# Attention scores as three split single-pass products, and the odd head's copy shared by two engines

## The chip, the cores and the metric

The kernel runs on one core of a Trainium2 chip. The metric is the device time of one execution in microseconds. All times below are microseconds unless ns is written. The engines are TensorE (PE; its weight loads are listed apart as PEld), VectorE (DVE), ScalarE (ACT), GpSimd (POOL) and SyncE (SP), which here only issues transfers.

## What is computed

Three layers in a row, all in fp32: attention with a learned bias by position, a layer with the maximum of three products, and a layer of eight experts. The change is in attention:

```python
B, H, S, D = 2, 8, 576, 64
scores = scale * np.matmul(q, k.transpose(0, 1, 3, 2))
scores = scores + bias.transpose(2, 0, 1)[None]      # bias[i, j, head], from a small net of i and j
scores = scores - np.max(scores, axis=-1, keepdims=True)
attn = np.exp(scores)
attn = attn / (np.sum(attn, axis=-1, keepdims=True) + 1e-09)
x = np.matmul(attn, v)                               # then: relu layer of 768, experts of 8 x 1024
```

## The kernel before

The program's order on every engine is the order in which the code is written. Three stages matter here.

**The bias stage** (12 to 68 us) runs 36 steps g16. In each, four tests `gen_s` make 0/1 tables for the step two ahead, shared out by the letters of `TESTS` (G is GpSimd, A ScalarE, V VectorE); `bias_mm` sums them on TensorE, `bias_ev` and `bias_out` scale them on VectorE, `bias_store` mirrors a part on ScalarE and stores it in DRAM. The tests have 12 buffers, three steps' worth.

**Attention** (68 to 196 us) takes the heads in pairs p = 0 to 3; a pair has nine units k, u = 9p + k, 36 in all. A unit is 128 rows of queries of one batch, for both heads of the pair: the even head x = 0 lies on partitions 0 to 63, the odd one on 64 to 127. For k = 8 the 64 left-over rows of both batches make one unit. One turn s of the loop does, in this order:

- `u_qk(s)`: the scores of both heads into two PSUM tiles sc (two buffers for two tiles: the next unit needs both of them read).
- `u_tr(s-1, 0)`: ten transposes of the even head's exponentials pe, 64x128 each, into the PSUM tile pt, of which there is one; `pv_part(s)`: a part of the product with v, by the table `PV`.
- `u_max(s, x)` on VectorE: scores plus bias and the row extreme, for both heads; `u_ev(s-1, 0)` on ScalarE: the copy of pt to SBUF (128x640).
- `u_exp(s, 0)`, a P·V copy `pv_ev` where the table `EV` has one (k = 0, 2 and 4 of the next pair), `u_exp(s, 1)`, all on ScalarE.
- `u_tr(s-1, 1)` and `u_ev(s-1, 1)`: the odd head's transposes into the same pt, and its copy on VectorE.
- at k = 0 `r_add` (VectorE: reciprocals of the row sums); their transpose `r_tr` on TensorE follows in the next turn ahead of the P·V part; `r_out` and `r_in` carry them through DRAM; at k = 6 and 7 `x_out` on GpSimd scales a batch of the output and splits it into xh and xl (three instructions each). Weight steps `w_step` (one instruction of VectorE, ScalarE or GpSimd each) run at k in `W_AT` of pairs 1 to 3.

The loads of q and k for the next pair are issued at k = 1, of v at k = 5, of the bias every second turn.

**After attention** TensorE runs the second layer (`m1_mm`), whose last chunk of x comes from pair 3 through `x_last`; `m1_first` fills its wait. Everything behind is the same in both kernels.

A matmul whose operands are of type fp32r is one instruction and one record in the trace. An fp32 matmul is one call, and two records.

Of the kernel before, what the change touches and what calls it, by code (L numbers as in the profile page):

```python
# [9 lines left out]
F32 = mybir.dt.float32  # L10
# [41 lines left out]
def make_body(stop=None):  # L52
    def body(tc, a):
# [21 lines left out]
        with ctx, tc.manual_schedule():  # L75
# [94 lines left out]
            qk_t, v_t = {}, {}  # L170
            bias_t = {}

            def load_qk(p):
                if p < H // 2:
                    qk_t[p] = hp_.tile([128, 2, B, S], F32, tag="qk", name="qk")
                    for part in range(2):
                        dma(qk_t[p][:, part], a["qk"][p][:, part])

# [18 lines left out]
            with ExitStack() as bctx:  # L197
# [126 lines left out]

                for g in range(8):
                    gen_s(g)
# [54 lines left out]
                for g16 in range(NG16):  # L381
                    ps = bias_mm(g16)
                    t = bias_ev(g16, ps)
                    for c in range(4):
                        if g16 + 2 < NG16:
                            gen_s(4 * (g16 + 2) + c)
                    bias_out(g16, ps, t)
                    if g16 == NG16 - 1:

                        A.activation(out=bc.tile([128, 1], F32, name="ex"), in_=ones[:, 0:1], func=AF.Exp)  # L390
                    for n in range(max(g16 - 1, 0), NG16 if g16 == NG16 - 1 else g16):
                        bias_store(n)
                    if g16 in (12, 20, 28):
                        load_bias((12, 20, 28).index(g16))
                    if g16 == 24:
                        load_v(0)

# [17 lines left out]
            with ExitStack() as actx:  # L415
# [13 lines left out]
                def u_qk(u):  # L429
# [3 lines left out]
                    q, kk = qk_t[p][:, 0], qk_t[p][:, 1]  # L433
                    for hf in range(2):
                        cs = slice(hf * SH, hf * SH + SH)
                        for x in range(2):
                            r = half[x]
                            if k < 8:
                                b, it = k % 2, k // 2
                                T.matmul(out=sc[x][:, hf, :SH], lhsT=q[r, b, 128 * it:128 * it + 128], rhs=kk[r, b, cs],  # L440
                                         start=True, stop=True)
                            else:
                                for b in range(B):
                                    T.matmul(out=sc[x][half[b], hf, :SH], lhsT=q[r, b, 512:576], rhs=kk[r, b, cs],
                                             start=True, stop=True)
# [17 lines left out]
                def u_exp(u, x):  # L463
                    p, k = divmod(u, 9)
                    c = 9 * x + U_COL[k]
                    pe = up.tile([128, S], F32, tag="pe", name="pe", bufs=6)
# [41 lines left out]
                def u_ev(u, x):  # L508
# [12 lines left out]
                    else:  # L521
                        V.tensor_copy(out=to, in_=src)
# [14 lines left out]
                def pv_ev(p, ch, b=None):  # L537
                    ps = pvs.pop(p)
                    if ch == 0:
                        x_t[p] = up.tile([128, B, S], F32, tag="x32", name="x32")  # L540
# [54 lines left out]
                for s in range(NU):  # L595
# [31 lines left out]
                    if k == 1:  # L627
                        load_qk(p + 1)
                    if k == 5:
# [630 lines left out]
def host_arrays(inp):  # L1260
# [3 lines left out]
    qk = np.stack([inp["q"], inp["k"]]).reshape(2, B, H // 2, 2, S, D).transpose(2, 3, 5, 0, 1, 4).reshape(H // 2, 128, 2, B, S)  # L1264
# [49 lines left out]
```

## Time and profile before

| | us |
|---|---|
| median of 3 runs (1066.9 to 1071.85) | 1067.08 |
| the profiled execution | 1065.98 |
| its span in the trace | 1064.2 |
| PE busy | 1040.0 (98%) |
| DVE busy | 756.7 (71%) |
| ACT busy | 560.8 (53%) |
| POOL busy | 313.7 (29%) |

The busy time of PE is modelled from pipelined matmuls, so 98% doesn't mean that every microsecond is needed. The chain of work that ended last lies on PE for 85% and on DVE for 9% of the span; of its lines L565, L1218 and L1133 (stages behind attention) have most, and the attention lines L534 (P·V), L440 (scores) and L506 (transposes) have 4%, 3% and 3%. From attention on PE is at 9 tenths or more in every slice of the span.

### The profile page before, as it was taken

The page shows a single profiled execution, that of the slowest core. Times are in us where ns is not written, and L with a number is a line of the kernel's source. Part 1 is how long each engine was busy: PE and PEld are TensorE (multiplying, and loading weights), DVE is VectorE, ACT ScalarE, POOL GpSimd, SP SyncE. Part 2 cuts the span into 40 slices and gives each one's busy share as a digit, 9 for nine tenths or more (in the row PEclk, how much of TensorE's full clock was granted, in tenths as well). Part 3 has the DMA queues.
Part 4 walks back from the last instruction along what each step waited for, and adds up shares of the span by engine and source line. Part 5 has one row for each costly group of instructions (what it writes and reads, how often), then busy time and mean ns, then how long its engine had stood idle before and what let it go on. Part 6 is the DMA issues. An engine that isn't in the chain of part 4 may idle for free.

```text
span 1064.2 us, 18893 instructions
## 1 busy us (share of the span) xinstructions
PE 1040.0 (98%) x7533; PEld 682.8 (64%) x7533; DVE 756.7 (71%) x1464; ACT 560.8 (53%) x922; POOL 313.7 (29%) x227
## 2 busy tenths in 40 slices
PE   7979999999999899999999999999999999999998
PEld 3246666899999666575665756657566475574653
DVE  7987777699968786877756667576675766757543
ACT  6977777345326656454454544545455454544530
POOL 6930323123206114344133141331412313223120
PEclk8999999999999999999999999999999999999999
DMA  4884673433441112203022030220302302110002
GB/s 150 261 270 149 190 223 89 141 120 119 82 139 41 33 31 65 65 21 85 20 66 65 20 85 21 65 68 32 71 23 63 83 22 66 27 39 6 2 1 89
DMA packets 39445, 85.31 MB, mean 80 GB/s; under 512 B 8052, under 2 KB 10300, under 8 KB 39356
## 3 DMA queue, kind: packets, MB, share of 16 engines
q1 hardware_dynamic: 39212, 83.81, 27.3%
q8 instruction: 59, 0.97, 0.4%
q10 hardware_dynamic: 144, 0.29, 0.1%
q14 instruction: 30, 0.25, 0.1%
HBM read 70.78 MB, written 13.30 MB: 79 GB/s over the span
## 4 chain that ended last, share of the span: by engine, by line
PE 85%; DVE 9%; ACT 3%; DMA 1%; issue 1%; POOL 0%; DVEq 0%; ACTq 0%
PE d L1218 33%; PE x L1133 12%; PE m L565 11%; PE y L1133 8%; PE z L1133 8%; PE pv L534 4%; PE sc L440 3%; PE pt L506 3%; PE p L343 1%; DVE bo L362 1%; PE o L984 1%; DVE s L1147 1%; DVE hl L1156 1%; DVE pk L711 1%; DMA bias_f<-bo 1%
## 5 line engine op out<-in xcount | busy, mean ns | idle before, releaser
L1218 PE MATMUL d<-w2h,hh 128*128 128x512 f16 x576 | 218.3, 379 | 0.8 <-DVE acc L1229 0.8
L1218 PE MATMUL d<-w2h,hl 128*128 128x512 f16 x576 | 218.3, 379 | 0.2 <-DVE hl L1156 0.2
L1218 PE MATMUL d<-w2l,hh 128*128 128x512 f16 x576 | 218.3, 379 | 0.0
L1133 PEld LDWEIGHTS <-w1h 128*128 128x128 f16 x1792 | 175.3, 98 | 49.7 <-issue 2.3
L1218 PEld LDWEIGHTS <-hh 128*128 128x128 f16 x1152 | 112.6, 98 | 132.9 <-issue 1.0
L1232 DVE SCALAR_TENSOR_TENSOR acc<-d,kh,acc 128x512 f32<-128x512 f32 x126 | 94.2, 748 | 93.6 <-PE d L1218 93.4
L864 POOL TENSOR_TENSOR w1l<-wf,w1h 128x768 f16<-128x768 f32 x32 | 53.6, 1676 | 359.2 <-ACT w1h L863 285.0
L1151 ACT ACTIVATE hh<-s 128x576 f16<-128x576 f32 x128 | 87.3, 683 | 128.5 <-DVE s L1147 100.9
L1156 DVE SCALAR_TENSOR_TENSOR hl<-s,hh 128x576 f16<-128x576 f32 x128 | 99.2, 776 | 47.5 <-ACT hh L1151 44.9
L867 ACT ACTIVATE w1h<-wf 128x1024 f16<-128x1024 f32 x32 | 33.8, 1056 | 132.2 <-DVE wf L860 132.2
L870 POOL TENSOR_TENSOR w1l<-wf,w1h 128x1024 f16<-128x1024 f32 x32 | 68.9, 2152 | 117.2 <-ACT w1h L867 117.2
L1133 PEld LDWEIGHTS <-w1l 128*128 128x128 f16 x896 | 87.9, 98 | 22.7 <-issue 0.4
L1218 PEld LDWEIGHTS <-hl 128*128 128x128 f16 x576 | 56.4, 98 | 68.5 <-DVE hl L1156 0.7
L1143 ACT ACTIVATE s<-x,cx 128x576 f32<-128x576 f32 x96 | 70.3, 733 | 28.6 <-PE x L1133 27.2
L945 POOL TENSOR_TENSOR w2l<-w2r,w2h 128x512 f16<-128x512 f32 x64 | 73.1, 1163 | 25.0 <-ACT w2h L944 25.0
L1133 PE MATMUL x<-xth,w1h 128*128 128x288 f16 x384 | 78.4, 286 | 0.6 <-ACT s L1143 0.6
L1133 PE MATMUL x<-xtl,w1h 128*128 128x288 f16 x384 | 78.6, 286 | 0.2 <-POOL xtl L875 0.2
L1133 PE MATMUL x<-xth,w1l 128*128 128x288 f16 x384 | 78.4, 286 | 0.0
L1147 DVE SCALAR_TENSOR_TENSOR s<-z,cx,s 128x576 f32<-128x576 f32 x64 | 52.3, 817 | 32.0 <-PE z L1133 25.2
L565 PE MATMUL m<-xh,wh 128*128 128x384 f32 x216 | 72.7, 337 | 0.0
L565 PE MATMUL m<-xl,wh 128*128 128x384 f32 x216 | 72.5, 336 | 0.0
L565 PE MATMUL m<-xh,wl 128*128 128x384 f32 x216 | 72.4, 335 | 0.0
(203 smaller groups left out, 1977.4 us busy)
## 6 DMA issues: line engine op xcount, KB each, us to landing
wr<-in_moe_w SPq DMA_DIRECT2D x50, 512.0 KB, 3.6
w2r<-in_moe_w SPq DMA_DIRECT2D x64, 256.0 KB, 2.8
bias_f<-bo SPq DMA_DIRECT2D x36, 295.5 KB, 4.0
bias<-bias_f SPq DMA_DIRECT2D x32, 288.0 KB, 3.2
qk<-in_qk SPq DMA_DIRECT2D x8, 576.0 KB, 6.2
wr<-in_moe_w_out SPq DMA_DIRECT2D x6, 512.0 KB, 3.9
v<-in_v SPq DMA_DIRECT2D x4, 640.0 KB, 4.5
bias<-bias_f SPq DMA_DIRECT2D x16, 144.0 KB, 4.2
```

Of the source, the lines that this page charges most:

```text
L534: T.matmul(out=to[half[x]], lhsT=v_t[p][:, x, b, j, :], rhs=pts[ch][:, x, j, b * w:b * w + w], start=(j == 0), stop=(j == 4))
L565: T.matmul(out=p[:, :TG], lhsT=ws[:, 128 * c:128 * c + 128], rhs=xs[:, c, TG * g:TG * g + TG], start=(c == 0 and n == 0), stop=(c == 3 and ...
L864: G.tensor_tensor(out=lo[:, 0:3], in0=t[:, 1:4], in1=hi[:, 0:3], op=ALU.subtract)
L870: G.tensor_tensor(out=lo[:, 3:7], in0=t[:, 4:8], in1=hi[:, 3:7], op=ALU.subtract)
L945: G.tensor_tensor(out=lo, in0=r, in1=hi, op=ALU.subtract)
L1133: T.matmul(out=ps[bank][:, s, :SH], lhsT=ws[:, i, c, :], rhs=xv[:, j, c, s * SH:s * SH + SH], start=(start and k == 0), stop=(k == 5), **kw)
L1143: A.activation(out=t, in_=src, func=AF.Identity, scale=c)
L1147: V.scalar_tensor_tensor(out=out, in0=z, scalar=scale, in1=out, op0=ALU.mult, op1=ALU.add)
L1151: A.activation(out=o, in_=src, func=AF.Relu)
L1156: V.scalar_tensor_tensor(out=l, in0=src, scalar=0.0, in1=o, op0=ALU.max, op1=ALU.subtract)
L1218: T.matmul(out=pd, lhsT=hs[:, fh, 128 * t:128 * t + 128], rhs=ws, start=(k == 0), stop=(k == 11))
L1232: V.scalar_tensor_tensor(out=acc[:, t, :], in0=pd, scalar=kh[:, 1 + t:2 + t], in1=acc[:, t, :], op0=ALU.mult, op1=ALU.add)
```

## The change

The scores are no longer fp32 products. q and k of a pair are split on the chip into a part that fits the single-pass type (h) and the rest (l), and a score is the sum of qh·kh, qh·kl and ql·kh. The parts of pair 0 are made in the bias stage: the h parts by ScalarE ahead of its tests, the l parts by GpSimd in four pieces of 576 columns after steps 11, 15, 19 and 23. Those of pair p + 1 are made by GpSimd at k = 2 to 5 of pair p. Left-over rows of batch 1 stand first in its q (the host lays them so) and 64 columns of zeros stand between the batches, so that the k = 8 unit sums two full products of 128 rows.

The odd head's copy out of pt is halved between VectorE and ScalarE. The P·V copies go from ScalarE to VectorE, behind the odd head's copy. The odd head's transposes and copy now stand ahead of `u_exp(s, 1)`. pe has 5 buffers (6 before), x32 one and qk one (2 before each); the parts have two.

```diff
@@ parts of q and k
+            def split_qk(p, part, low, bs=slice(0, B), on_act=False):
+                if p < H // 2:
+                    if p not in hl_t:
+                        hl_t[p] = [[hp_.tile([128, B, w], F32R, tag=t + x, name=t + x) for t, w in (("q", 640), ("k", S))] for x in "hl"]
+                        for x in range(2):
+                            G.memset(raw(hl_t[p][x][0][:, 0, S:]), 0.0)
+                    hi, lo = (t[part][:, bs, :S] for t in hl_t[p])
+                    src = qk_t[p][:, part, bs]
+                    if low:
+                        G.tensor_tensor(out=lo, in0=src, in1=raw(hi), op=ALU.subtract)
+                    elif on_act:
+                        A.activation(out=hi, in_=src, func=AF.Copy)
+                    else:
+                        pool_copy(hi, src)
...
+                for part in range(2):
+                    split_qk(0, part, False, on_act=True)
+                pieces = [(0, part, True, slice(b, b + 1)) for b in range(B) for part in range(2)]
                 for g in range(8):
                     gen_s(g)
...
+                    if g16 % 4 == 3 and 7 < g16 < 24:
+                        split_qk(*pieces.pop(0))
@@ u_qk
-                    q, kk = qk_t[p][:, 0], qk_t[p][:, 1]
+                    hi, lo = hl_t[p]
+                    b, it = k % 2, k // 2
+                    mm = [(b, 704 * b + 128 * it)] if k < 8 else [(0, 512), (1, 576)]
+                    mm = [(q.rearrange("p b c -> p (b c)")[:, c:c + 128], kk[:, b]) for b, c in mm
+                          for q, kk in ((hi[0], hi[1]), (hi[0], lo[1]), (lo[0], hi[1]))]
                     for hf in range(2):
-                        cs = slice(hf * SH, hf * SH + SH)
-                        for x in range(2):
...
-                                T.matmul(out=sc[x][:, hf, :SH], lhsT=q[r, b, 128 * it:128 * it + 128], rhs=kk[r, b, cs],
-                                         start=True, stop=True)
...
+                        for y, (q, kk) in enumerate(mm):
+                            for x in range(2):
+                                T.matmul(out=sc[x][:, hf, :SH], lhsT=q[half[x]], rhs=kk[half[x], hf * SH:hf * SH + SH],
+                                         start=(y == 0), stop=(y == len(mm) - 1))
@@ u_ev, odd head
-                        V.tensor_copy(out=to, in_=src)
+                        V.tensor_copy(out=to[:, :, 0], in_=src[:, :, 0])
+                        A.activation(out=to[:, :, 1], in_=src[:, :, 1], func=AF.Copy)
@@ pv_ev
-                        A.activation(out=x_t[p][:, :, 0:256], in_=ps.rearrange("p (b i) -> p b i", b=2), func=AF.Copy)
+                        V.tensor_copy(out=x_t[p][:, :, 0:256], in_=ps.rearrange("p (b i) -> p b i", b=2))
...
-                        A.activation(out=x_t[p][:, b, 256:576], in_=ps[:, :320], func=AF.Copy)
+                        V.tensor_copy(out=x_t[p][:, b, 256:576], in_=ps[:, :320])
@@ one turn
                     u_exp(s, 0)
-                    for n, e in in_turn(EV, s):
-                        pv_ev(n, *e)
-                    u_exp(s, 1)
                     if s > 0:
                         u_tr(s - 1, 1)
                         u_ev(s - 1, 1)
+                    u_exp(s, 1)
+                    for n, e in in_turn(EV, s):
+                        pv_ev(n, *e)
...
                     if k == 1:
                         load_qk(p + 1)
+                    if 1 < k < 6:
+                        split_qk(p + 1, k // 2 - 1, k % 2 == 1)
```

In the order of TensorE's instructions, the place around unit 8 (k = 8 of pair 0), before; sc are score tiles, pt the transposes, pv the product with v, and "x4" that one instruction stands four times:

```order
L440 MATMUL sc<-qk 128x288 x4
L506 MATMUL pt<-ident,pe 128x64 x10
L534 MATMUL pv<-pt_1513,v 64x256 x4
L506 MATMUL pt<-ident,pe 128x64 x10
L444 MATMUL sc<-qk 64x288 x8
L506 MATMUL pt<-ident,pe 128x64 x10
L534 MATMUL pv<-pt_1513,v 64x256 x4
```

The scores of unit 8 after (the same place; qh, ql, kh, kl are the parts):

```order
L523 MATMUL pt<-ident,pe 128x64 x10
L461 MATMUL sc<-kh,qh 128x288 x2
L461 MATMUL sc<-kl,qh 128x288 x2
L461 MATMUL sc<-kh,ql 128x288 x2
L461 MATMUL sc<-kh,qh 128x288 x2
L461 MATMUL sc<-kl,qh 128x288 x2
L461 MATMUL sc<-kh,ql 128x288 x2
L461 MATMUL sc<-kh,qh 128x288 x2
L461 MATMUL sc<-kl,qh 128x288 x2
L461 MATMUL sc<-kh,ql 128x288 x2
L461 MATMUL sc<-kh,qh 128x288 x2
L461 MATMUL sc<-kl,qh 128x288 x2
```

The last row of them, one more ql, is left out. A usual unit has the first six such rows, 12 matmuls, where it had 4 fp32 calls; unit 8 has twelve rows, 24 matmuls, where it had 8 calls on quarters of the array.

VectorE at the turn k = 0 of pair 1, before (ISA is the reduction of `u_max`, with its accumulator read; rt and st the row sums; ww a weight step):

```order
L457 ISA ng,st<-sc,bias 128x576
L457 ISA st 128x1
L522 COPY pt_1514<-pt 128x10x64
L477 TENSOR_SCALAR rt<-st 128x6x3
L478 RECIPROCAL st<-rt 128x18
L124 TENSOR_SCALAR ww<-ww 128x4x128
L457 ISA ng,st<-sc,bias 128x576
```

and after:

```order
L474 ISA ng,st<-sc,bias 128x576
L474 ISA st 128x1
L539 COPY pt_1526<-pt 128x5x64
L559 COPY x_2044<-pv 128x2x256
L494 TENSOR_SCALAR rt<-st 128x6x3
L495 RECIPROCAL st<-rt 128x18
L124 TENSOR_SCALAR ww<-ww 128x4x128
L474 ISA ng,st<-sc,bias 128x576
```

The copy is half as wide, and the P·V copy x stands between it and the reciprocals; the next unit's reduction is behind all of them. ScalarE around the same turn, before:

```order
L520 ACTIVATE pt_1514<-pt 128x10x64
L467 ACTIVATE pe,st<-ng,st 128x576
L541 ACTIVATE x_1911<-pv 128x2x256
L467 ACTIVATE pe,st<-ng,st 128x576
L110 ACTIVATE ww<-wr 128x4x128
```

and after:

```order
L537 ACTIVATE pt_1526<-pt 128x10x64
L484 ACTIVATE pe,st<-ng,st 128x576
L540 ACTIVATE pt_1526<-pt 128x5x64
L484 ACTIVATE pe,st<-ng,st 128x576
L110 ACTIVATE ww<-wr 128x4x128
```

Half of the odd head's copy now stands between the two exps in every turn, and the P·V copy is gone.

## Rows read from the trace of the kernel before

**Rows 1.** Stage table, core 0: length, busy of PE, PEld, DVE, ACT, POOL (instructions), clock, DMA

```profile
93.00:123.00 30.00, 30.00 (x348) 18.53 (x344) 22.34 (x51) 22.61 (x52) 6.51 (x6) 1.00 0.61 183
```

**Rows 2.** Timeline of a unit: start, length, engine, line, operation, tiles [idle before <-releaser]

```profile
83.17 0.80 PEld L440 LDWEIGHTS sc<-qk 64*128 64x128 f32 x8
...
83.43 0.82 DVE L522 COPY pt<-pt 128x640 f32<-128x640 f32 x1 [0.30 <-PE pt L506]
...
84.37 0.42 PEld L506 LDWEIGHTS pt<-ident,pe 64*128 64x128 f32 x10 [0.41 <-ACT pe L467]
...
84.56 0.76 DVE L457 CUSTOM_DVE_ANT_0 ng<-sc,bias 128x576 f32<-128x576 f32 x1 [0.30 <-PE sc L440]
...
84.86 0.63 PEld L534 LDWEIGHTS pv<-pt,v 128*64 128x64 f32 x8
...
84.97 0.70 ACT L520 ACTIVATE pt<-pt 128x640 f32<-128x640 f32 x1 [0.65 <-PE pt L506]
...
85.24 0.75 DVE L457 CUSTOM_DVE_ANT_0 ng<-sc,bias 128x576 f32<-128x576 f32 x1
...
85.57 0.77 ACT L467 ACTIVATE pe<-ng,st 128x576 f32<-128x576 f32 x1
...
85.87 0.39 PEld L506 LDWEIGHTS pt<-ident,pe 64*128 64x128 f32 x10 [0.39 <-ACT pt L520]
...
86.17 0.79 PEld L440 LDWEIGHTS sc<-qk 64*128 64x128 f32 x8
...
86.44 0.82 DVE L522 COPY pt<-pt 128x640 f32<-128x640 f32 x1 [0.43 <-PE pt L506]
```

**Rows 3.** Chain that ended last, in order of time: start, length, what

```profile
110.70 1.77 PE pv L534 x12
...
181.63 1.13 PE sc L444 x16
...
195.71 109.58 PE m L565 x630
...
310.86 9.69 PE o L984 x72
```

**Rows 4.** Groups by form, 0 to 420 us: count | busy, mean ns | idle before

```profile
L543 ACT ACTIVATE x<-pv 128x320 f32<-128x320 f32 x6 | 2.6, 437 | 1.9 <-PE pv L534 1.9
...
L132 ACT ACTIVATE wh<-ww 128x512 fp32r<-128x512 f32 x18 | 11.3, 630 | 18.8 <-DVE ww L130 18.7
...
L130 DVE SCALAR_TENSOR_TENSOR ww<-wr,ww 128x512 int32<-128x512 int32 x24 | 16.9, 704 | 0.7
...
L551 POOL TENSOR_TENSOR xl<-x,xh 128x576 fp32r<-128x576 f32 x6 | 8.5, 1415 | 0.5
...
L62 POOL TENSOR_SCALAR xh<-x 128x576 fp32r<-128x576 f32 x6 | 4.4, 735 | 0.5
```

**Rows 5.** Timeline at k = 0 of pair 2, VectorE

```profile
129.71 0.27 DVE L478 RECIPROCAL st<-rt 128x18 f32<-128x18 f32 x1
```

**Rows 6.** Stage table in steps of 1 us, columns as in rows 1

```profile
9.00:10.00 1.00, 0.00 (x0) 0.00 (x0) 0.93 (x4) 1.00 (x3) 1.00 (x1) 0.50 0.00 0
```

**Rows 7.** Timeline of the bias stage's start, ScalarE's tests

```profile
9.02 2.69 ACT L318 ACTIVATE s<-rs,nthr 128x564 f16<-128x564 f16 x4
...
14.70 1.37 ACT L318 ACTIVATE s<-rs,nthr 128x528 f16<-128x528 f16 x2 [3.00 <-DVE t L352]
```

**Rows 8.** Timeline of the bias stage, GpSimd's tests and VectorE's first reading of step 13

```profile
30.00 1.21 POOL L321 TENSOR_SCALAR s<-rs,thr 128x372 f16<-128x372 f16 x1 [0.27 <-PE p L343]
...
34.86 0.59 DVE L352 SCALAR_TENSOR_TENSOR t<-p,ics,tab 128x372 f32<-128x372 f32 x1
...
38.20 15.92 POOL L321 TENSOR_SCALAR s<-rs,thr 128x324 f16<-128x324 f16 x12 [0.22 <-PE p L343]
```

**Rows 9.** Timeline at the end of attention, the last P·V copy on ScalarE

```profile
187.51 0.60 ACT L541 ACTIVATE x<-pv 128x512 f32<-128x512 f32 x1 [0.38 <-PE pv L534]
```

**Rows 10.** DMA issues by line: count, KB each, median us to landing

```profile
qk<-in_qk SPq DMA_DIRECT2D x8, 576.0 KB, 6.2
```

More of the change, by code (lines that the diff above doesn't have):

```diff
@@ L168, in body @@
             hp_ = hctx.enter_context(pool("heads", bufs=2))
-            qk_t, v_t = {}, {}
+            qk_t, v_t, hl_t = {}, {}, {}
             bias_t = {}
@@ L174, in load_qk @@
                 if p < H // 2:
-                    qk_t[p] = hp_.tile([128, 2, B, S], F32, tag="qk", name="qk")
+                    qk_t[p] = hp_.tile([128, 2, B, S], F32, tag="qk", name="qk", bufs=1)
                     for part in range(2):
                         dma(qk_t[p][:, part], a["qk"][p][:, part])
+            def split_qk(p, part, low, bs=slice(0, B), on_act=False):
[12 more added lines that the diff above has]
+                        pool_copy(hi, src)
             def load_v(p):
@@ L432, in u_qk @@
                     un[u] = {"sc": sc, "pe": []}
-                    q, kk = qk_t[p][:, 0], qk_t[p][:, 1]
-                    for hf in range(2):
-                        cs = slice(hf * SH, hf * SH + SH)
-                        for x in range(2):
-                            r = half[x]
-                            if k < 8:
-                                b, it = k % 2, k // 2
-                                T.matmul(out=sc[x][:, hf, :SH], lhsT=q[r, b, 128 * it:128 * it + 128], rhs=kk[r, b, cs],
-                                         start=True, stop=True)
[L442 to L445, printed above, removed]
+                    hi, lo = hl_t[p]
[3 more added lines that the diff above has]
+                          for q, kk in ((hi[0], hi[1]), (hi[0], lo[1]), (lo[0], hi[1]))]
+                    for hf in range(2):
+                        for y, (q, kk) in enumerate(mm):
+                            for x in range(2):
+                                T.matmul(out=sc[x][:, hf, :SH], lhsT=q[half[x]], rhs=kk[half[x], hf * SH:hf * SH + SH],
+                                         start=(y == 0), stop=(y == len(mm) - 1))
                 st_t = {}
@@ L465, in u_exp @@
                     c = 9 * x + U_COL[k]
-                    pe = up.tile([128, S], F32, tag="pe", name="pe", bufs=6)
+                    pe = up.tile([128, S], F32, tag="pe", name="pe", bufs=5)
                     A.activation(out=pe, in_=un[u].pop(("ng", x)), func=AF.Exp, bias=st_t[p][:, 0, c:c + 1], scale=-1.0,
@@ L539, in pv_ev @@
                     if ch == 0:
-                        x_t[p] = up.tile([128, B, S], F32, tag="x32", name="x32")
-                        A.activation(out=x_t[p][:, :, 0:256], in_=ps.rearrange("p (b i) -> p b i", b=2), func=AF.Copy)
+                        x_t[p] = up.tile([128, B, S], F32, tag="x32", name="x32", bufs=1)
+                        V.tensor_copy(out=x_t[p][:, :, 0:256], in_=ps.rearrange("p (b i) -> p b i", b=2))
                     else:
-                        A.activation(out=x_t[p][:, b, 256:576], in_=ps[:, :320], func=AF.Copy)
+                        V.tensor_copy(out=x_t[p][:, b, 256:576], in_=ps[:, :320])
                 def x_out(p, b):
@@ L1262, in host_arrays @@
     c = np.ascontiguousarray
-    qk = np.stack([inp["q"], inp["k"]]).reshape(2, B, H // 2, 2, S, D).transpose(2, 3, 5, 0, 1, 4).reshape(H // 2, 128, 2, B, S)
+    q = np.stack([inp["q"][0], np.concatenate([inp["q"][1][:, 512:], inp["q"][1][:, :512]], 1)])
+    qk = np.stack([q, inp["k"]]).reshape(2, B, H // 2, 2, S, D).transpose(2, 3, 5, 0, 1, 4).reshape(H // 2, 128, 2, B, S)
     v = inp["v"].reshape(B, H // 2, 2, S, D)
```

## The prediction

> **What bounds the kernel now.** First the stage table. The change touches the bias stage (12 to 68 us) and attention (68 to 196 us); behind them 870 us run on as they are, with TensorE full. In attention no engine is full: VectorE and ScalarE work 22.3 and 22.6 of 30 us at a granted clock of 1.00, and TensorE's 30.00 is modelled [rows 1]. So the limit is a ring of waits, and the timeline of one unit shows it [rows 2]. One PSUM tile pt serves both heads. T is the load of the odd head's transposes (85.87). Its copy starts 0.57 later (86.44, VectorE, 0.82 long), and the next even transposes load 0.12 after a copy ends (83.43 + 0.82 = 84.25, then 84.37): 0.57 + 0.82 + 0.12 = 1.51 us. From there 0.49 to the P·V product (84.86) and 1.01 to the next T (85.87): 3.01 us a unit. Two other rings are nearly as long. TensorE's own: the scores load 0.30 after T (86.17) and hold the array until the even transposes, 1.20 later (83.17 to 84.37), which is the same 1.5. That of the score tiles: load 83.17, first reduction 84.56, second 85.24, done at 86.0, next load 86.17: 2.83 to 3.0. An edit that shortens one of the three alone gains next to nothing; this one shortens all three.
>
> **The scores.** Before, a unit is 4 fp32 products, 8 records in the trace. What a column costs follows from two full-array fp32r streams: 630 matmuls of 384 columns in 109.58 us are 0.174 each, 72 of 288 in 9.69 are 0.135, so 96 columns cost 0.039 us, 0.41 ns a column, and the rest is 0.015 a matmul [rows 3]. That products on array halves run in pairs shows at P·V: 12 records of 320 columns at two passes would be 12 x 0.262 = 3.1 us in a row, and took 1.77 [rows 3]. By the same reckoning the old scores are 4 rounds of 2 x 288 columns, 0.95 us plus a little. The new unit is 12 single-pass matmuls of 288 columns, 6 rounds of two: 6 x 0.135 = 0.81, at least 6 x 0.12 = 0.72. That no load shows between them rests on the transposes: ten loads of 64x128 fit into the 0.30 us between 85.87 and 86.17, five to a half, 0.06 each, under the 0.12 that a matmul streams [rows 2]. TensorE's part behind T falls from 0.36 + 0.95 to 0.36 + 0.81 = 1.17.
>
> The Trainium skill speaks against this. "TensorE: Matmul & The Clock Gate", section "LDWEIGHTS (loading the stationary operand)", gives a load by its columns, so an estimate of 107 ns for 128, and its Part 3 on packing small matmuls lets a load overlap a running matmul only in another row group. By that a round would be 0.107 + 0.12, six of them 1.36, and the scores would be dearer than before; the sum would be the second rival's. Its first figure is not what the ten loads of rows 2 show; the second is not decided by any row with short matmuls.
>
> **The odd head's copy.** VectorE and ScalarE take half each. ScalarE's 128x320 takes 0.44 [rows 4] against 0.70 for 640 [rows 2]; in that ratio VectorE's 0.82 becomes 0.51. ScalarE starts later than VectorE behind transposes (84.37 to 84.97 is 0.60 for the even ones), but must first end the even head's exp, which starts at 85.57 and takes 0.77, so it is free before T + 0.57. So this path is 0.57 + 0.51 + 0.12 = 1.20, or 0.60 + 0.44 + 0.12 = 1.16 on ScalarE: I take 1.18, level with TensorE's 1.17. A unit with P·V goes from 3.01 to 2.68, 0.33 less. Bound: if the scores keep their 0.95, 0.36 + 0.95 = 1.31 and the gain is 0.20. There are 27 such units (5 to 35 without the four k = 8): **-8.9**, bound -5.4. Units 1 to 4 have no P·V and follow the ring of the score tiles; it loses about 0.26 of scores and hand-over: **-1.0**, bound -0.5.
>
> **The k = 8 units.** They ran 16 records on quarters in 1.13 us [rows 3], and now run 24 on halves: 12 x 0.135 = 1.62, against 0.95 of four rounds on quarters. TensorE is then ready at T + 0.36 + 1.62 = 1.98; before, 0.36 + 1.13 = 1.49 lay under the ring's 1.51. So +0.47 each, **+1.9** for four, bounds +1.2 (12 x 0.12) and +2.4.
>
> **What lands on VectorE and ScalarE instead.** ScalarE per unit: even copy 0.60 (84.97 to 85.57), two exps of 0.77, half a copy 0.34 to its successor: 2.5 of 2.68 us. VectorE: reductions 0.68 + 0.76, half copy 0.47: 1.9. So both have little room, and what came beside them free before now shows. At each k = 0 (three times) VectorE does the P·V copy of 512 columns behind its half copy (some 0.65, from 0.82 for 640), then the reciprocals of the row sums (0.27 [rows 5], some 0.38 with the add ahead of them), and in two pairs a weight step of 0.43 to 0.70. The next scores are ready at T + 1.35; VectorE is free at T + 1.04 + 0.65 + 0.38 = 2.07, with the step at 2.5 to 2.75. The transposed reciprocals make TensorE wait too (r_tr stands ahead of P·V). I get +0.3 to +0.8 at each of the three: **+1.6**, bounds 0 and +3. The two 320-column P·V copies, 0.4 each, mostly fit the 0.3 of slack: **+0.3**. The weight steps elsewhere (VectorE 0.70, ScalarE 0.63 [rows 4]) find 0.1 to 0.3 of slack at units with short P·V: five of them cost 0.2 to 0.4, with smaller ones **+2.0**, bounds 0 and +3.
>
> **Bias stage.** Two ScalarE copies of 1,152 columns stand ahead of its tests: by the step from 0.44 to 0.70 us for 320 more columns, 1.13 each, 2.3 in all. The q and k loads are in by then, as the DMA share is 0.00 from 9 us [rows 6], so ScalarE ends its four tests (2.69, from 9.02) at 14.0. It idled 3.00 us until 14.70 [rows 7]: nothing. GpSimd gets four subtractions of 1.41 [rows 4]. It has 0.27 of idle a step up to 38 us and none behind (12 tests in 15.92) [rows 8], so a part of the 5.7 us stays as lateness, some 3.4 us at the fourth. The cover is the lead of the tests: that of step 13 (372 columns) is done at 31.21 and VectorE first reads what comes of it at 34.86 [rows 8], 3.65 us later, of which its own matmuls take a part: about 3. What passes it meets a wait of VectorE that is there anyway. **+0.3**, bounds 0 and, with the cover gone at the last two, +2.6.
>
> **Later pairs' parts** cost GpSimd 2 x 1.47 + 2 x 2.8 = 8.6 us a pair (twice the 0.73 and 1.41 of [rows 4]), with x_out's 7.1 behind: 15.7 of some 27 us. Nothing, unless it is late (below). The loads keep their place on SP's queue; the single qk buffer is read out a pair earlier. The pads are set once per pair by GpSimd, hidden.
>
> **The end of attention.** The last P·V copy moves ahead of the reciprocals on VectorE (before, 0.60 from 187.51 on ScalarE [rows 9]), and r_tr, which stood ready right behind the transposes, waits for it: **+0.7**, bounds 0 and +0.9. Everything behind keeps its distance.
>
> **Sum.** -8.9 - 1.0 + 1.9 + 1.6 + 0.3 + 2.0 + 0.3 + 0.7 = -3.1 us from the profiled execution's 1065.98 (span 1064.2 and 1.8 around it): 1062.9. The median shown is 1067.08, 1.1 above that execution; I give 1063.5, between 1062.9 and 1064.0. With all good bounds it is -8.7 (1058 on the median's footing), with all bad ones +6 (1073).
>
> **Rivals.**
> 1. *The added work hides after all.* The +1.6, +2.0 and +0.3 rest on slacks of 0.1 to 0.3 us. If VectorE and ScalarE catch up within a unit, as they did before, the sum is -7.0, and -7.7 with the k = 8 units at the low bound: about 1059.5, and 1057 if the scores are at 0.72 and the copies keep pace with them. For it: long P·V units leave 0.4 to 0.8 us to catch up. Against it: ScalarE at 2.5 of 2.68.
> 2. *Loads show (slower).* A load into a half waits until that half's matmul is through. A round is then 0.12 + 0.06 = 0.18 from the ten loads, or 0.12 + 0.10 from the eight of the old scores (0.79 us merged at 83.17). Six rounds are 1.08 to 1.32, T + 1.44 to 1.68 against 1.51: a unit gains 0.07 or loses 0.17 (-1.9 to +4.6 over 27), a k = 8 unit takes 1.0 to 1.5 more (+4.0 to +6.0), and with +4.9 from the other terms it is +7 to +15.5: 1074 to 1082. It decides once a round is above 0.15. For it: no row has so short a matmul behind a load on the same half. Against it: the two fp32r streams hide a full-array load behind 0.12 us of streaming. It is the skill's overlap rule made a mechanism.
> 3. *GpSimd is late.* With one x32 buffer VectorE's P·V copy at k = 0 waits until x_out of the pair before is through. From the qk issue: 6.2 us landing [rows 10], 8.6 of parts, 7.1 of x_out is 21.9, against some 23.5 to the copy. If GpSimd runs a tenth slower and the load lands a microsecond late, it is 0.9 to 1.5 late at two boundaries: +2 to +3, 1066.
> 4. *It doesn't do what it says*: the halves don't pair in this form. Twelve in a row are 1.62, T + 1.98: +0.47 x 27, +2.1 x 4, +5: above 1085.
>
> **How the numbers follow.** Forecast 0.50, the first rival 0.26, the second 0.12, the third 0.09, the fourth 0.03. A measurement of this kernel can tell about 0.5% from no change, 5.3 us: faster is below 1061.7, slower above 1072.4. The forecast's own spread puts 0.12 of its 0.50 below 1061.7 and 0.02 above 1072.4; so faster 0.12 + 0.26 = 0.38, slower 0.02 + 0.12 + 0.03 = 0.17, same 0.45. The range 1055.5 to 1071.5 takes in nearly all of the forecast, rival 1 with 1.5 us below its 1057 (the spread of the before runs is larger), and rival 3; it leaves out 2 and 4 and some of the tails.
>
> **What would show it.** In the profile after: units of 2.7 us with 8 P·V records of 256 columns; score loads to even transposes in about 1.0 instead of 1.20, and about 1.7 at k = 8; the half copies at 0.44 and 0.5; ScalarE over 85% busy in attention; units k = 1 longer than the others by 0.3 to 0.8, with VectorE's reduction starting late; the bias stage's end at 68.0 to 68.5; granted clock 1.00 as before. It is wrong if score rounds take more than 0.15 us, if the bias stage ends above 70, or if a P·V copy waits for GpSimd.

## The result and the profile after

| | before | after |
|---|---|---|
| median, us | 1067.57 (6 runs, 1066.55 to 1071.85) | 1075.26 (6 runs, 1074.25 to 1077.05) |
| profiled execution, us | 1065.98 | 1075.98 |
| its span and mean granted clock | 1064.2, 0.991 | 1074.2, 0.984 |
| load of the first scores, us | 67.96 | 68.14 |
| load of unit 6's scores, us | 86.17 | 90.17 |
| start of the 630 matmuls behind attention, us | 195.71 | 205.80 |

The ratio is 1.0061, 95% interval 1.0044 to 1.0079: slower by 0.6%. The forecast was 1063.5, at most 1071.5. In the two profiles all of the loss has come by the end of attention, as the 630 matmuls that started at 195.71 [rows 3] start 10.1 us later and take as long as before. (The profiled execution of before is one of its shorter ones, so this is more than the 6.5 us of the ratio.) The chain that ended last, after (start, length, what):

```profile
205.80 109.47 PE m L583 x630
```

The stage table of after for the stretch of [rows 1] (columns as there) has VectorE at 18.76 us for 22.34, ScalarE at 22.94 for 22.61, GpSimd at 9.32 for 6.51. VectorE gave work away, and no engine is full. The limit is still a ring of waits:

```profile
93.00:123.00 30.00, 27.51 (x367) 19.05 (x365) 18.76 (x49) 22.94 (x55) 9.32 (x8) 1.00 0.58 171
```

One unit of after in its timeline, to be laid beside [rows 2] (start, length, engine, line, operation, tiles, idle before and what ended it):

```profile
155.93 0.39 PEld L523 LDWEIGHTS pt<-ident,pe 64*128 64x128 f32 x10 [0.39 <-ACT pt L537]
...
156.23 0.20 PEld L461 LDWEIGHTS sc<-kh,qh 64*128 64x128 f32 x2
...
156.35 0.19 PEld L461 LDWEIGHTS sc<-kl,qh 64*128 64x128 f32 x2
...
156.48 0.18 PEld L461 LDWEIGHTS sc<-kh,ql 64*128 64x128 f32 x2
156.50 0.49 DVE L539 COPY pt<-pt 128x320 f32<-128x320 f32 x1 [0.39 <-PE pt L523]
...
157.02 0.44 ACT L540 ACTIVATE pt<-pt 128x320 f32<-128x320 f32 x1 [0.51 <-DVE pt L539]
...
157.51 0.39 PEld L523 LDWEIGHTS pt<-ident,pe 64*128 64x128 f32 x10 [0.44 <-ACT pt L540]
```

Here stands the answer. L539 and L540 copy the two halves of one PSUM tile. VectorE begins 0.57 behind T (155.93 to 156.50), as forecast, and its half takes 0.49, as forecast. ScalarE has been idle for 0.51 us, and what releases it is VectorE's copy: its half begins 0.03 after the other's end and takes 0.44. TensorE then waits for ScalarE. T to the next even transposes is 157.51 - 155.93 = 1.58 us, longer than the 1.51 of before; forecast was 1.18. A unit without further work takes 3.05 us for 3.01.

What else adds up is in the chain of the same profile, at a pair's later units and at the end of attention:

```profile
159.51 1.64 PE sc L461 x24
...
170.60 0.75 ACT pe L484 x2
171.35 0.16 ACT rt L504
...
171.56 1.84 PE pv L552 x12
...
181.93 0.75 ACT pe L484 x2
182.68 0.52 ACT wh L132
183.20 0.60 ACT pt L537
...
196.75 0.69 DVE x L559
...
197.55 0.28 DVE st L495
...
197.87 0.28 PE pv L500
```

The 24 matmuls of a k = 8 unit take 1.64 us, against 1.13 [rows 3] and a forecast of 1.62. At 170.60 ScalarE stands in the chain with the second exp and the copy of the transposed reciprocals (L504), because its half copies made it late (experiment 2 shows it); P·V at k = 2 waits for that. At 181.93 it is exp, weight step (L132) and even copy in a row. At 196.75 the end of attention waits for VectorE's P·V copy, the reciprocals and their transposes, as the forecast's last term said.

The granted clock is the other thing that differs between the two profiles. Of TensorE's two levels, 1.2 and 2.4 GHz, it had the lower between 70 and 90 us. The stage table of after, then that of before, same stretch (the last three numbers of a row are clock, DMA share, GB/s):

```profile
70.00:90.00 20.00, 16.60 (x164) 14.24 (x166) 9.87 (x27) 13.69 (x31) 7.55 (x4) 0.50 0.64 202
```

```profile
70.00:90.00 20.00, 16.68 (x190) 11.74 (x192) 14.01 (x33) 14.73 (x33) 0.00 (x0) 0.91 0.73 244
```

Units 2 to 4 take 3.67 us each in that stretch. That looks like 4.0 us of the 10.1 (unit 6 starts at 90.17 for 86.17); experiments 3 and 4 show that this reading of two single profiles would have misled.

### The profile page after: what moved, and what is told of

It reads as the page before. It is cut to its first block, busy times and chain, and to the rows that moved or that the text cites. A ratio compares the mean times of both kernels' runs of the same rounds, so it can differ in the third digit from the quotient of the medians.

```text
span 1074.2 us, 19251 instructions
## 1 busy us (share of the span) xinstructions
PE 1035.9 (96%) x7693; PEld 694.8 (65%) x7693; DVE 750.2 (70%) x1474; ACT 570.8 (53%) x950; POOL 342.2 (32%) x251
## 4 chain that ended last, share of the span: by engine, by line
PE 76%; DVE 6%; ACT 3%; issue 1%; POOL 0%; DVEq 0%
PE d L1238 33%; PE x L1153 12%; PE m L583 11%; PE y L1153 8%; PE z L1153 8%; PE pv L552 2%; PE o L1004 1%; PE pt L523 1%; DVE hl L1176 1%; DVE s L1167 1%; DVE pk L731 1%; ACT hh L1171 1%; DVE t L905 1%; ACT s L1163 0%; DVE pt L539 0%
```

## The experiments

The theory: the forecast's rings are right, and its one wrong step is that the two half copies run side by side; made to do so, the unit falls to what was forecast. The rivals: ScalarE is too full anyway; the split scores are what costs; the low granted clock is what costs.

### 1. Two PSUM tiles, so that the halves can overlap

In the instruction order with its waits, ScalarE's half of the odd head's copy in the changed kernel waits for a semaphore of VectorE (DVE_49):

```
L540 ACTIVATE pt_1526<-pt 128x5x64 [waits DVE_49]
```

With a tile of its own for each 64-row half, the same copy (L538) waits for one of TensorE (PE_49) alone.

```diff
-pt = un[u]["pt"] = ps_t.tile([128, 2, 512], F32, tag="pt", name="pt")
+pt = un[u]["pt"] = [ps_t.tile([128, 512], F32, tag=f"pt{i}", name=f"pt{i}") for i in range(2)]
...
+for i in range(2):
+    src = un[u]["pt"][i][:, :320].rearrange("p (j n) -> p j n", n=64)
+    if x == 0 or i == 1:
+        A.activation(out=to[:, :, i], in_=src, func=AF.Copy)
+    else:
+        V.tensor_copy(out=to[:, :, i], in_=src)
...
```

> The transposes' PSUM tile pt is two tiles of one bank, one for each 64-row half of a score tile, so that VectorE and ScalarE read different tiles when they copy the odd head; the even head's copy becomes two ScalarE instructions. Theory A (the only thing that failed is that ScalarE's half of the odd copy stood behind VectorE's half, 0.50 + 0.45 in a row where 0.50 was forecast): the half copies overlap, the span from the load of the odd transposes to the next even ones falls from 1.56 to 1.2 us, and a plain unit falls from 3.05 to 2.8 (the even copy in two pieces, 0.45 each for 0.70, gives 0.1 to 0.2 back). 27 units: 5 to 8 us off 1075.3, 1067 to 1070. Rival B (ScalarE takes the place of the wait: two exps of 0.77, three half copies of 0.45 are 2.9 us a unit): the halves overlap but units stay at 2.9 to 3.05, 1071 to 1075.

Measured: 1068.72 us, ratio to before 0.9998 (0.9978 to 1.0017), some 6.5 us less than after. Its timeline:

```profile
91.85 0.39 PEld L523 LDWEIGHTS pt<-ident,pe 64*128 64x128 f32 x10 [0.39 <-ACT pt L538]
...
92.41 0.49 DVE L540 COPY pt<-pt 128x320 f32<-128x320 f32 x1 [0.28 <-PE pt L523]
92.45 0.44 ACT L538 ACTIVATE pt<-pt 128x320 f32<-128x320 f32 x1
...
93.02 0.42 PEld L523 LDWEIGHTS pt<-ident,pe 64*128 64x128 f32 x10
...
93.59 0.77 ACT L538 ACTIVATE pt<-pt 128x320 f32<-128x320 f32 x2
...
94.53 0.39 PEld L523 LDWEIGHTS pt<-ident,pe 64*128 64x128 f32 x10 [0.39 <-ACT pt L538]
```

The halves lie at 92.41 to 92.90 and 92.45 to 92.89, and the next even transposes load at 93.02, 1.17 behind T (91.85) where the forecast had 1.18. Units of the plain kind take 2.67 us (92.16, 94.83 and so on), where the forecast had 2.68. Theory A holds. Rival B falls: ScalarE does all this in 2.67 us, since the even copy in two pieces takes 0.77 together, hardly more than the 0.69 in one.

The change could not have had this by itself: the two halves of its one tile lie in different PSUM banks, as the two tiles of the edit do, but the program's wait goes by the tile. The Trainium skill, "PSUM — Partial Sum Buffer", section "PSUM bank collisions raise a hardware error", says why such waits are put in at all: two engines must not touch one bank and partition quadrant at once, reads against reads included, while different banks run clean. The overlap at 92.41 agrees with the second; no run here shows a collision.

### 2. The even head's copy shared as well, and the odd head's not shared at all

```diff
-    if x == 0 or i == 1:
+    if i == 1:
```

> As the run with two one-bank tiles, and the even head's copy is shared too: VectorE takes the first half, ScalarE the second, of both heads. ScalarE then has 2 x 0.77 + 2 x 0.45 = 2.44 us a unit, VectorE 2 x 0.72 + 2 x 0.50 = 2.44. Theory A: units fall to 2.6 to 2.75 us, 8 to 12 us off 1075.3: 1063 to 1067. Rival B (the even copy's half waits on VectorE behind the two reductions, which stand ahead of it): the even copy ends later than ScalarE's whole copy did, units at 2.9 to 3.1, 1071 to 1076.

Measured: 1088.98 us, ratio 1.0199 (1.0173 to 1.0225), far above either theory's range; rival B's mechanism is what the timeline shows:

```profile
93.57 0.44 ACT L538 ACTIVATE pt<-pt 128x320 f32<-128x320 f32 x1
...
94.00 0.75 DVE L474 CUSTOM_DVE_ANT_0 ng<-sc,bias 128x576 f32<-128x576 f32 x1
...
94.68 0.48 DVE L540 COPY pt<-pt 128x320 f32<-128x320 f32 x1
...
95.28 0.42 PEld L523 LDWEIGHTS pt<-ident,pe 64*128 64x128 f32 x10 [1.19 <-ACT pe L484]
```

ScalarE's half is over at 94.01. VectorE's stands behind both reductions and ends at 95.16, and the odd transposes load at 95.28 (94.53 in experiment 1's kernel, whose unit began 0.05 later). A unit takes 3.48 us. Dividing work evenly over two engines doesn't help where the queue of one puts its share behind something else.

The other direction, from the changed kernel, gives VectorE the whole odd copy:

```diff
-V.tensor_copy(out=to[:, :, 0], in_=src[:, :, 0])
-A.activation(out=to[:, :, 1], in_=src[:, :, 1], func=AF.Copy)
+V.tensor_copy(out=to, in_=src)
```

> The odd head's copy is one VectorE instruction of 640 columns again; all else as in the changed kernel. Theory A (the shared copy is no help because its halves run one after the other, 0.95 for 0.82, and it loads ScalarE by 0.45 a unit, which shows at the units with P.V copies' hand-overs and weight steps): plain units go from 3.05 back to 3.01 and those at k = 1, 2, 5 lose 0.2 to 0.4 of their excess, 2 to 5 us off 1075.3: 1070 to 1073. Rival B (ScalarE's load isn't what makes those units long, it is r_add and the P.V copies on VectorE): VectorE with 0.3 more a unit gets them longer still, 1075 to 1078.

Measured: 1072.77 us, ratio 1.0043 (1.0027 to 1.0059): theory A. The plain unit is at 3.00 to 3.01 again, and those at k = 2 are back at 3.76 from 4.25 to 4.52; they were long because of ScalarE's half copies, while r_add and the P·V copy of k = 0, behind a whole copy of 0.82 on VectorE, make those at k = 1 3.87. So the split, one half after the other, cost some 2.5 us.

### 3. The scores alone

From the changed kernel, scores are four fp32 products again and no parts of q and k are made.

```diff
-for y, (q, kk) in enumerate(mm):
-    for x in range(2):
-        T.matmul(out=sc[x][:, hf, :SH], lhsT=q[half[x]], rhs=kk[half[x], hf * SH:hf * SH + SH],
-                 start=(y == 0), stop=(y == len(mm) - 1))
+T.matmul(out=sc[x][:, hf, :SH], lhsT=q[r, b, o:o + 128], rhs=kk[r, b, cs], start=True, stop=True)
...
```

> The scores are four fp32 products again (16 at k = 8), and the parts of q and k aren't made; copies and the order of the rest as in the changed kernel. Theory A (the three split products shorten nothing in a plain unit, because the ring through the transposes' tile is longer; they cost 0.5 us at each k = 8 and, since TensorE has less to do in the first seven units, the granted clock stays at 0.50 until 90 us): plain units stay at 3.05, k = 8 units lose 0.5 each, the granted clock is back at 1.00 by 76 us; 2 + 4 = 6 us off 1075.3, 1069. Rival B (the low clock until 90 us doesn't depend on the scores): 2 us off, 1073. Rival C (the split scores do shorten units): plain units 3.1 to 3.2 and 1076 or more.

Measured: 1072.69 us, ratio 1.0053 (1.0032 to 1.0074), 2.6 less than after, the time of rival B. Plain units stay at 3.05, so rival C falls, and in the profiled execution the granted clock is 0.50 from 69 until past 85 us, split scores or not. How much of the 2.6 is due to the scores the times don't show: the four executions with a mean granted clock of 0.991 or more average 1070.9 us, but the four at 0.985 to 0.987 average 1075.4, as much as after's six, which lie at 0.984 to 0.988. In the two profiles, both at 1.00 there, units 7 to 34 take 95.87 us for 96.93 of after, 1.1 less; two of the three k = 8 units among them are 0.5 shorter, the third 0.1. The chain of this kernel:

```profile
89.85 1.03 PE sc L457 x8
...
95.95 1.13 PE sc L462 x16
```

Four fp32 products take 1.03, where the forecast had 0.95 for them; the twelve split ones take 0.85 in the chain of experiment 1's kernel, forecast 0.81. The price of the scores was right to 0.1 us, and nothing came of it in a plain unit, since a longer ring stood over it.

### 4. The granted clock

Matmuls that nobody reads were added in two places, behind the bias stage's last ones and in the first units (below for the changed kernel; in the kernel before one fp32 product stands for the four).

```diff
+pf = pb[0].tile([128, 2, 512], F32, tag="p", name="pf")
+for _ in range(8):
+    T.matmul(out=pf[:, 1, :], lhsT=wz[:, :128], rhs=wz, start=True, stop=True)
...
+def fill():
+    pf = ps_v.tile([128, 512], F32, tag="pv", name="pf")
+    for _ in range(4):
+        T.matmul(out=pf, lhsT=hl_t[0][0][0][:, 0, :128], rhs=hl_t[0][0][1][:, 0, :512], start=True, stop=True)
...
 u_qk(s)
+if s in (0, 1):
+    fill()
 if s > 0:
     u_tr(s - 1, 0)
+if s in (1, 2, 3, 4):
+    fill()
```

> The changed kernel with matmuls added whose result nobody reads: eight bf16 ones of 512 columns behind the bias stage's last, and four single-pass ones of 512 columns (0.85 us at full clock) behind the scores of units 0 and 1 and in P.V's place in units 1 to 4. Theory A (the granted clock falls to 0.50 at 70 us because TensorE idles before the first scores, and stays there until 90 us because the first units give it too little): it stays at 1.00, units 1 to 5 take 3.05 us instead of 3.67, and the scores of unit 6 load at 86.2 to 86.7 instead of 90.17: 3.5 to 4 us off 1075.3, 1071.5. Rival B (the clock falls whatever TensorE does there): the low stretch stays and the added matmuls cost up to 2 us, 1075 to 1078.

> The kernel before with the same added matmuls (in the units one fp32 product of 512 columns in place of four single passes). Theory A: its low stretch, 72.2 to 76 us, goes too, and unit 2 takes 2.9 us instead of 3.81: 0.9 us off, ratio 0.999. If the kernel before is often longer in that low stretch than its one profile shows, more, up to 4 us (0.996). Rival B (the added matmuls only cost): ratio 1.000 to 1.002.

> The changed kernel with only the eight added matmuls behind the bias stage's last, none in the units. Theory A1 (TensorE's idle stretch ahead of the first scores alone brings the clock down): it stays at 1.00 and unit 6 loads its scores at 86 to 87.5; 1071.5 to 1072.5. Theory A2 (what the first units do decides): the clock is at 0.50 from 70 to 74 us on, until 85 to 90; 1074 to 1076.

> The changed kernel with only the added matmuls in units 0 to 4, none behind the bias stage. Theory A1 (the idle stretch ahead of the first scores brings the clock down, and work in the units only brings it back sooner): 0.50 from 70 us, back at 1.00 by 75 to 80; 1072.5 to 1074. Theory A2 (what the first units do decides): 1.00 throughout, 1071.5 to 1073.

| | us | ratio to before |
|---|---|---|
| after, both fillings | 1072.78 (1072.43 to 1073.71) | 1.0041 (1.0025 to 1.0056) |
| before, both | 1065.82 (1064.95 to 1066.52) | 0.9975 (0.9963 to 0.9987) |
| after, only behind the bias stage | 1072.56 (1070.28 to 1075.86) | 1.0044 (1.0027 to 1.0061) |
| after, only in the units | 1073.73 (1072.03 to 1074.25) | 1.0042 (1.0023 to 1.0062) |

Stage tables of TensorE (length, busy and records; clock, DMA share, GB/s): first after itself, then with both, then with the filling behind the bias stage alone, then with that in the units alone.

```profile
66.00:68.00 2.00, 0.57 (x20) 1.00 0.89 226
...
70.00:74.00 4.00, 2.99 (x24) 0.50 0.89 273
```

```profile
66.00:68.00 2.00, 2.00 (x37) 1.00 0.68 173
...
70.00:74.00 4.00, 3.92 (x30) 1.00 0.88 251
```

```profile
66.00:68.00 2.00, 2.00 (x30) 1.00 0.88 226
...
74.00:78.00 4.00, 2.69 (x46) 1.00 0.95 368
78.00:82.00 4.00, 3.18 (x42) 0.63 0.48 128
82.00:86.00 4.00, 3.20 (x38) 0.50 0.60 197
```

```profile
66.00:68.00 2.00, 0.68 (x24) 1.00 0.85 217
...
70.00:74.00 4.00, 4.00 (x18) 0.57 0.90 277
74.00:78.00 4.00, 3.72 (x48) 1.00 0.99 362
```

In these profiles both theories of the last two runs are half right. In after, where TensorE was busy for 0.57 of 2 us ahead of the first scores, the clock falls at 70. With that stretch filled and the units thin, it holds until 79 and falls then, until 90. With the stretch left open and the units filled, it falls at 70 and is back within 4 us. With both filled it stays at 1.00 throughout. A single profile doesn't stand for all executions, though. With the filling behind the bias stage alone, five of ten have a mean granted clock of 0.993 to 0.996 and average 1071.1 us, and five have 0.987 to 0.990 and average 1074.9. And the kernel before, with 0.23 of the same 2 us, had the low clock from 72 to 76 only:

```profile
66.00:68.00 2.00, 0.23 (x10) 1.00 0.82 217
...
72.00:74.00 2.00, 1.12 (x18) 0.65 0.99 393
74.00:76.00 2.00, 2.00 (x14) 0.50 1.00 401
```

But the last word on the clock's share is the second row of the table. The kernel before gains 0.25% from the same filling, and its times then lie within 1.6 us of each other. Its 70 executions beside these experiments show why: 34 have a mean granted clock of 0.983 to 0.987 and 19 one of 0.992 or more, and the 15 at 0.986 average 1070.2 us, the 10 at 0.992 average 1066.0. So, by these means, the kernel before has a long low stretch in about half of its executions; the one that was profiled, at 0.991, had only some 4 us of it. The changed kernel's six lie at 0.984 to 0.988. With both kept at 1.00 the change costs 1072.78 - 1065.82 = 7.0 us, no less than the 0.6% without filling. The low clock is a cost of both kernels, and it doesn't explain the loss. That the change adds a little to it is not excluded: of the 44 executions of kernels with split scores and no filling 34 have a mean of 0.987 or less, of the 80 with fp32 scores and no filling 38. In the filled pair the first scores come 1.6 us later, 0.2 in the pair without filling, and that could hide a share of some 1 us.

### 5. What the end and GpSimd cost, and the best version

From experiment 1's kernel, VectorE makes the reciprocals ahead of the 512-column P·V copy, each k = 0 and at the end:

```diff
+if s > 8 and k == 0:
+    r_add(p - 1)
 for n, e in in_turn(EV, s):
     pv_ev(n, *e)
...
+r_add(NP - 1)
 pv_part(NU)
 pv_ev(NP - 1, 0)
-r_add(NP - 1)
...
```

> The run with two one-bank tiles pt, and the reciprocals of the row sums ahead of the 512-column P.V copy on VectorE, at each k = 0 and at the end of attention. Theory A (the forecast's term for the end was the transposes of the reciprocals waiting behind that copy; it showed as 1.4 us): 1.2 to 1.5 us at the end, 0 to 0.4 at each of three k = 1 units, 1.5 to 2.5 us off that run's 1068.7: 1066.2 to 1067.2. Rival B (something else at the end, the transposes of the last unit or the load of the reciprocals' rows, ends as late): 0 to 0.5 us off, 1068.2 to 1068.7.

Measured: 1066.43 us, ratio 0.998 (0.9965 to 0.9996), 2.3 less: theory A. From the load of the first scores to the 630 matmuls it takes 129.6 us (68.23 to 197.82) for 131.2 (67.83 to 199.01) in two profiles of the same mean clock, 0.986, so 1.6 of the 2.3 are seen there.

The three edits together:

> Two one-bank tiles pt, the reciprocals first, and the added matmuls, all three together. If the three gains are independent: 1068.7 less 2 less 4 is 1062.7, ratio to the kernel before 0.994. If the low clock can't be filled away: 1066.5 to 1068, ratio 0.998 to 1.000.

Measured: 1060.97 us, ratio 0.9934 (0.9914 to 0.9953). The gains add, and give 3 us more than the single runs promise (1075.26 less 6.5, 2.3 and 2.5 is 1064.0). Why was not tested; the kernels of experiment 1 and of the reciprocals lay at a low mean clock in most executions, 0.982 to 0.987, which may have hidden a part of their gain. In its profiled execution one unit still stood out, in the timeline at k = 5 of pair 2:

```profile
140.41 2.63 POOL L188 TENSOR_TENSOR kl<-qk,kh 128x1152 fp32r<-128x1152 f32 x1
140.49 2.83 DVE L124 TENSOR_SCALAR ww<-ww 128x512 f32<-128x512 f32 x1
...
144.05 0.18 PEld L465 LDWEIGHTS sc<-kh,qh 64*128 64x128 f32 x1 [1.87 <-DVE st L478]
```

VectorE's weight step, 0.43 elsewhere, begins 0.08 behind GpSimd's subtraction and ends 0.28 after it; the reductions queue behind it and the scores wait 1.87 us. The changed kernel has the same at 150.21, where L124 takes 1.97 beside the subtraction of 149.25. The kernel before has it too, at another place: L125 of 146.70 takes 1.23 beside GpSimd's multiplication of 146.23. So the weight steps of attention were moved:

```diff
-W_AT = (0, 2, 4, 5, 7)
+W_AT = {1: (0, 1, 4, 5, 7, 8), 2: (0, 1, 2, 4, 7, 8), 3: (0, 2)}
...
-if k in W_AT:
+if k in W_AT[p]:
```

> The run with all three edits, and the weight steps of attention moved so that VectorE's two single-source ones (lines 124 and 125) don't fall where GpSimd subtracts the parts of q and k or multiplies x; in that run the one at 140.49 us took 2.83 us instead of 0.43 beside GpSimd's subtraction (140.41, 2.63 long), and the next scores waited 1.9 us. Theory A (VectorE's step can't run while GpSimd's two-source instruction does): every such step takes 0.43 again and units 23 to 25 lose 1.5 to 2.4 us: 1058.5 to 1060 against 1061.0. Rival B (the step was long for another reason, or what it hid comes out elsewhere): 1060.5 to 1061.5.

Measured: 1059.45 us, ratio 0.9917 (0.9896 to 0.9938), the best of all and within theory A. Both single-source steps of pair 2 are short again, in VectorE's timeline:

```profile
130.54 0.42 DVE L124 TENSOR_SCALAR ww<-ww 128x512 f32<-128x512 f32 x1
...
134.69 0.42 DVE L125 TENSOR_SCALAR ww<-ww 128x512 int32<-128x512 int32 x1
```

Last, what the split scores are worth once the halves run side by side; the kernel of all three edits (not the moved weight steps) with fp32 scores:

> The run with all three edits, but its scores are four fp32 products again and no parts are made. Theory A (the forecast's reckoning: with the halves of the copy parallel, TensorE's part, 0.36 + 0.95, becomes the longest and a plain unit takes 2.81 instead of 2.67; k = 8 units lose 0.5, and GpSimd no longer holds VectorE up): 24 plain units + 3, four k = 8 units - 2, the held-up weight step - 1.5 to - 2.4, in all 1059.5 to 1061. Rival B (the split scores are worth more than that, units 2.9): 1062.5 to 1064. Rival C (plain units don't need them, 2.70): 1057.5 to 1059.

Measured: 1061.16 us, ratio 0.9931 (0.9912 to 0.995), 0.2 above theory A's range and the nearest to it. The chain:

```profile
88.80 1.03 PE sc L461 x8
89.83 0.31 PE pt L528 x10
90.14 1.01 PE pv L557 x8
91.15 0.45 PE pt L528 x10
91.61 1.13 PE sc L466 x16
```

The chain runs on TensorE alone, and a plain unit takes 2.80 to 2.88 us, where the forecast's bound (scores at 0.95) was 2.81. The first k = 8 unit takes 2.91 us for 3.46. The two effects and GpSimd's hold-up nearly cancel: 1061.16 against 1060.97. With the hold-up gone the split scores are worth some 1061.16 - 1059.45 = 1.7 us; the weight steps stand at other places in these two kernels, and what that alone makes no run tells apart.

## Why the prediction was wrong

To keep the clock out, the terms are laid against the two filled kernels of experiment 4 (both at 1.00 from the first scores on), whose 630 matmuls start at 196.52 and 203.87. First before, then after:

```profile
196.52 109.47 PE m L569 x630
```

```profile
203.87 109.47 PE m L587 x630
```

| part | forecast | measured |
|---|---|---|
| to the first scores | +0.3 | 67.27 to 68.91: +1.6 |
| units 0 to 5 | -1.0 | 19.04 to 19.21: +0.2 |
| units 6 to 34 | -8.9 + 1.4 + 1.6 + 0.3 + 2.0 = -3.6 | 96.06 to 100.20: +4.1 |
| unit 35 and the end of attention | +0.5 + 0.7 = +1.2 | 14.15 to 15.55: +1.4 |
| sum | -3.1 | +7.35 |

- **Units with P·V, forecast -8.9: wrong, and nearly all of the miss.** The failed step is "VectorE and ScalarE take half each", with a path of 0.57 + 0.51 + 0.12. Each duration in it was right (0.57, 0.49, 0.44). That both engines can read the tile at once was assumed, and ScalarE's wait for VectorE, which stands in the order of the changed kernel's instructions, was not looked for. The path became 0.57 + 0.49 + 0.44 and hand-overs, 1.58, and a plain unit grew by 0.04 to 0.05 where it was to lose 0.33. Apart from the units named below that makes +0.4, 9.3 above forecast. With the wait gone the unit took 2.67 for a forecast of 2.68 (experiment 1).
- **Units 1 to 4, forecast -1.0: not seen.** In the filled pair these units wait for the half copies as well: with the same filling and the halves side by side (the kernel of all three edits) units 2 to 4 take 2.77 to 2.84 us, against 3.05 to 3.11 in the filled kernel before and 3.16 to 3.23 in the filled changed one. Without filling, at 1.00, no run shows them.
- **k = 8, forecast +1.9 for four: right.** 1.64 for 1.13 in the chain; the three among units 6 to 34 grew by 1.6 in all, forecast 1.4.
- **k = 0's work and the P·V copies, forecast +1.6 and +0.3: right in sum, by luck.** Units at k = 1 and 2 grew by 0.5 and 1.5 over three pairs. The larger part, at k = 2, had another cause, ScalarE's late copy of the transposed reciprocals, and it was gone in experiment 2 when VectorE had the whole odd copy.
- **Weight steps, forecast +2.0, bound 0: too high, and one mechanism missed.** Units at k = 5 grew by 1.9 in all, but those at k = 6 and 7 shrank by 1.8. Of the 1.9 one half is the unit in which L124 runs beside GpSimd's subtraction. The forecast had put GpSimd's parts at "nothing, unless it is late". It was not late, it was in VectorE's way. But so was the x_out of the kernel before, as its filled run shows at k = 6 of pair 1: VectorE's weight step L128 of 116.83 takes 1.89 beside GpSimd's subtraction of 116.76 (1.41 long). In the filled changed kernel, where x_out comes later, that step (120.21) takes 0.68, and this unit and the next are 0.6 shorter each. So the change moved such meetings, it didn't bring the first ones in.
- **Bias stage, forecast +0.3, bound +2.6: in the bounds, larger than taken.** In the two profiles without filling it was +0.2.
- **End of attention, forecast +0.7: right**, +0.9 beside the last k = 8 unit's 0.5.

The test of the whole sum is experiment 1's kernel at equal clock: its three executions at 0.986 average 1067.7, 2.5 below the 1070.2 of the kernel before, and its two at 0.993 average 1063.9, 1.9 below the 1065.8 of before's five. (Its median is no lower than before's because ten of its twelve executions have a mean clock of 0.987 or less.) So the forecast of -3.1 was good to about 1 us for a kernel whose halves overlap, and the changed kernel isn't that kernel.

Of the rivals, loads between short matmuls (the second) and halves that don't pair (the fourth) are refuted by twelve matmuls in 0.85 us: 0.14 a round. Rounds begin 0.13 apart in after's unit (156.35, 156.48), and a matmul's 288 columns take some 0.12 of that by the prediction's estimate from [rows 3], so a load into the same half can't have waited for it. The overlap rule weighed in the prediction doesn't hold here, and row and not rule decided rightly. GpSimd's lateness (the third) showed nowhere: none of the P·V copies of 512 columns waits for it. The first, all added work hidden, didn't come: the added work showed, if not always where it was forecast. The time fell into the second's range of 1074 to 1082 by a mechanism that none of the four named; "it doesn't do what it says" had been drawn up for the matmuls and not for the copy. None of the three signs that the prediction gives for being wrong came true either, since none looks at the waits between the half copies.

The forecast of the clock, "1.00 as before", came from one profile at 0.991. That one execution was on the good side of a spread that the kernel before has by itself.

## What to carry to other kernels

Before work on one tile is credited to two engines in parallel, look at the waits of the changed program: if the second engine's instruction waits for the first's, the split is a series, and a tile for each engine is the remedy. An engine that gets "free" work on the side must be laid against what its neighbour does at that time, instruction by instruction, since two engines can hold each other up without any wait in the program; moving such work can bring a meeting in at one place and take one away at another. And a stretch of low clock that one profile shows and the other doesn't is no effect of the change until the clocks of many executions, or a filled control, say so.

## What the runs showed of the hardware

- VectorE's single-source step of 128x512 fp32 took 2.83 us instead of 0.43 when it was issued 0.08 behind GpSimd's two-source subtraction of 2.63, and 1.97 when issued 0.96 behind one of 2.64; each time it ended about 0.3 after GpSimd. The Trainium skill, "SBUF — State Buffer", section "Who interferes with whom", has this as an exclusive lock on a port pair that the two share, by which whoever comes first holds it for its whole instruction; the two rows agree. A step with two sources was held up too, the L128 of 116.83 above (1.89 for 0.68). VectorE's copies out of PSUM of 149.40 and 156.50 in after were not: they lie inside GpSimd's two-source instructions (149.25, 2.64 long, and 155.73, 1.41 long) and take their 0.49.
- Twelve single-pass products on array halves, 128 stationary and 288 moving columns each, took 0.85 us with a load of their own each, and 24 took 1.64 to 1.68.
- The granted clock fell to 0.50 at the seam of two stages and stayed there for 20 us in which TensorE was busy for 16.60 (70 to 90 in after). It was back within 4 us when matmuls were put into that work. In the kernel before a long low stretch comes, by the mean clocks, in about half of its executions, and those at 0.986 take 4.2 us more than those at 0.992, as much as many a change is worth.
